# A scan ahead of routed experts: y products with two heads as moving columns, and routing steps spread over other pairs

## The chip, the cores and the metric

The kernel runs on one core of a Trainium2 chip. The metric is the device time in microseconds. A core has five engines with a queue each: TensorE (PE; its weight loads are listed as PEld), VectorE (DVE), ScalarE (ACT), GpSimd (POOL) and SyncE (SP), which here only issues DMAs. The trace gives for any stretch the clock that TensorE was granted, as a share of 2.4 GHz: 1.00 is 2.4 GHz, 0.50 is 1.2 GHz, and what lies between is a stretch that saw both.

## The reference, cut to what matters

```python
# part 1: a chunked state-space scan; x (4, 8, 768, 32), B and C (4, 8, 768, 16), a (4, 8, 768)
cum = np.cumsum(log(a) in the chunk, axis=-1)
M = (Cc @ Bc.T) * exp(cum_i - cum_j) * causal
y = M @ xc + (Cc @ state) * exp(cum)          # intra + inter
state = exp(sum) * state + sum_j Bc_j * exp(cum_last - cum_j) * xc_j
# part 2: tokens (3072, 256) = y of all heads side by side; 8 experts
expert_idx = token_ids * 2654435761 % 8
out[mask_e] = relu(x[mask_e] @ w1[e]) @ w2[e]  # w1 (8, 256, 1024), w2 (8, 1024, 256)
```

## The kernel before

**The scan.** Sequences are cut into units of T = 64 tokens. A pair k covers 256 tokens of one batch (four units, two chunks of 128); there are 12 pairs, three to each of four batches. In a prologue the decays are made (`fac`), B and C are multiplied by them (`rows_part`), transposed on PE (`turn_bc`) and brought back to SBUF (`evict_bc`, as `bts` for B and `ces` for C; `ces` has two copies, in each of which the other head of a pair of heads is zero). `back(k)` transposes B once more for the states, `dstates` makes the state's growth of each unit in PSUM, `states` adds it up on DVE (`z`) and writes the scaled state on POOL (`sps`). `gram(k)` makes the products of C and B in PSUM, and `masked(k)` copies their causal part into SBUF (`m_sb`, two copies on DVE).

**The y products.** `inter(k, swap)` (L561) multiplies `ces` by the state, `intra(k, t)` (L571) `m_sb` by x. Both take one head at a time: 32 moving columns a matmul, and each fp32 matmul runs as two passes, so that the trace shows twice as many. All of a pair's y lies in two PSUM banks (BY and BY + 1), from which `y_evict` (L578) copies it in one ACT instruction; `y_store` sends it to `y_tokens` in DRAM.

**Order in a pair.** The loop over k issues: loads of x, B and C; the store of pair k - 1; `turn_bc` and `evict_bc` of the next batch; `inter(k, 0)`, `dstates` and `states` of pair k + 1, `intra(k, 0)`, again `dstates` and `states`, `intra(k, 1)`; `rows_part` of a later batch on POOL; `inter(k, 1)`, `y_evict(k)`, `gram(k + 1)`, `piece(k)`, `back(k + 2)`, `masked(k + 1)`. Each engine runs its instructions in this order, which nothing rearranges.

**Routing.** `piece(k)` holds a step of the routing of tokens to experts: mask and count of tokens (`rt_mask`, `rt_count`, pair 0), ranks of experts and sizes (`rt_prefix`, pair 1; `rt_place`, `rt_rank`, pair 2), slots (`rt_slot_*`, pairs 3 and 4), then in quarters the one-hot table of lanes (`rt_lanes`, L390, 24 instructions on POOL), the one-hot table of slot tiles (`rt_tiles`, DVE) and their product on PE (`rt_table`, L404), and the list of token numbers (`to_index`). At the end of pair 9 POOL issues the indirect gathers of the five early token tiles (`gather`, L448), and PE turns three of them at the end of pair 10 and two at the end of pair 11 (`turn_x`, L456). The halves of w1 of the first experts are loaded by SP in pairs 8 to 10.

**The experts** follow (`up`, `down`, `sums_*`, `put`); the change does not touch them. `filler(n)` (L177) issues n bf16 products of zeros with 512 columns into an unused bank; `ident` is the identity for PE's transposes.

Of the kernel before, what the change touches and what calls it, by code (L numbers as in the profile page):

```python
# [25 lines left out]
def kernel(  # L26
# [148 lines left out]
    def filler(n):  # L175
        for _ in range(n):
            pe.matmul(out=ps[:, 3], lhsT=fill16[:, 0:P], rhs=fill16, start=True, stop=True)  # L177
# [19 lines left out]
    filler(3)  # L197
# [28 lines left out]
    def evict_bc(b, part, bank, eng):  # L226
        k = 0
        for i, r0, r1 in PARTS[part]:
            src = ps[:, bank, k * P:(k + r1 - r0) * P].rearrange("q (r p) -> q r p", p=P)
            k += r1 - r0  # L230
            if i == 0:
                o = bts[b].rearrange("q (p r) -> q r p", r=R)[:, r0:r1]
# [5 lines left out]
            for e in range(2):  # L238
                o = ces[b][:, e].rearrange("q (p r) -> q r p", r=R)[:, r0:r1]
                if eng[e] is act:  # L240
# [31 lines left out]
    def rt_ids():  # L272
# [4 lines left out]
        pe.transpose(out=ps[:, BQ, 0:NCH], in_=eid_r, identity=ident[0:NCH, 0:NCH])  # L277
        dve.tensor_copy(out=eid, in_=ps[:, BQ, 0:NCH])
# [31 lines left out]
    def rt_place(n, poh):  # L310
        pick = small("pick", [P, 3, E, E])
        for i in range(3):
            dve.tensor_tensor(out=pick[:, i], in0=poh, in1=ctab[:, i].unsqueeze(1).to_broadcast([P, E, E]), op=OP.mult)
        dve.tensor_reduce(out=sel, in_=pick, axis=AX.X, op=OP.add)
        who = small("who", [P, E, E])
        dve.tensor_tensor(out=who, in0=poh.rearrange("q e k -> q k e"), in1=iota_e.unsqueeze(1).to_broadcast([P, E, E]),
                          op=OP.mult)
        whof = small("whof", [P, E])
        dve.tensor_reduce(out=whof, in_=who, axis=AX.X, op=OP.add)
        dve.tensor_copy(out=place_i, in_=whof)  # L320
        half = sel[:, 0]
# [12 lines left out]
        dve.tensor_tensor(out=ovt, in0=tend, in1=ovt, op=OP.subtract)  # L334
        dve.tensor_scalar(out=ovt, in0=ovt, scalar1=float(P), scalar2=float(NSL), op0=OP.mult, op1=OP.add)
        dve.scalar_tensor_tensor(out=ovt, in0=half, scalar=-2.0, in1=ovt, op0=OP.mult, op1=OP.add)
        dve.tensor_tensor(out=ovt, in0=ovt, in1=sel[:, 1], op=OP.subtract)
        dve.tensor_tensor(out=ovt, in0=ovt, in1=sel[:, 2], op=OP.subtract)
# [42 lines left out]
    CG = 6  # L381

    def rt_lanes(eng, q):
        c = slice(q * CG, (q + 1) * CG)
        if eng is dve:
            dve.tensor_tensor(out=laneoh[:, c], in0=iota_n.unsqueeze(1).to_broadcast([P, CG, P]),
                              in1=lane[:, c].unsqueeze(2).to_broadcast([P, CG, P]), op=OP.is_equal)
            return
        for i in range(q * CG, (q + 1) * CG):
            eng.tensor_scalar(out=laneoh[:, i], in0=iota_n, scalar1=lane[:, i:i + 1], scalar2=None, op0=OP.is_equal)  # L390
# [214 lines left out]
    dstates(0, 1)  # L605
    masked(0)
    states(0, (1, 2, 3))
    back(1)

    state = {}  # L610

# [434 lines left out]
```

## Time and profile before

| | us |
|---|---|
| three runs: median (lowest to highest) | 316.12 (312.74 to 316.29) |
| the profiled execution, its own time | 310.52 |
| its span, first to last instruction | 308.8 |
| TensorE's mean granted clock over the span | 0.834 |
| PE busy, PEld busy | 262.1, 233.7 |
| DVE, ACT, POOL busy | 171.0, 85.7, 190.3 |

A busy PE is not a PE at its peak, since matmuls are pipelined and their ends are modelled; what a row of matmuls takes is read from the starts of its first and of what follows it. The share of busy time is a mean over a prologue, a scan and an expert part that have different limits. In the rows below a name with two arrows is output<-input, and what stands in square brackets is the idle time ahead of the instruction and who ended it.

### The profile page before, as it was taken

To read this page: it belongs to the slowest core of one execution; us is meant where nothing else is said; L and a number is where in the kernel's file an instruction comes from. 1 tells how busy PE (TensorE), PEld (TensorE's weight loads), DVE (VectorE), ACT (ScalarE), POOL (GpSimd) and SP (SyncE) were. 2 spreads that over 40 slices of the span, in tenths; PEclk is the share of its full clock that TensorE was granted. 3 is DMA by queue.
4 is the path that set the end of the run, shared out by engine and by line. 5 is a ranking of instruction groups with operands and counts; after the bars stand their busy time and mean duration, and the time that the engine had idled before them with its cause. 6 is when DMAs were issued, how large, how long until landed. Compare 5 with 4: busy or idle time off the path is not lost.

```text
span 308.8 us, 8166 instructions
## 1 busy us (share of the span) xinstructions
PE 262.1 (85%) x3373; PEld 233.7 (76%) x3374; DVE 171.0 (55%) x343; ACT 85.7 (28%) x183; POOL 190.3 (62%) x240
## 2 busy tenths in 40 slices
PE   8559968899899897888899899699699899999840
PEld 3338747787678686768889899699699898999730
DVE  6542673855343104796666647775763866656420
ACT  4412532234411246031112140141142240332100
POOL 3423366689927228989849739869359589272440
PEclk9755995559655569797999999799799999999985
DMA  8913474335544359350370551280170140410110
GB/s 185 219 23 70 89 157 102 58 75 101 114 112 126 106 139 363 111 187 3 88 269 20 175 167 34 46 312 18 20 269 20 65 142 17 152 38 17 51 41 14
DMA packets 55098, 33.30 MB, mean 108 GB/s; under 512 B 34906, under 2 KB 49394, under 8 KB 55060
## 3 DMA queue, kind: packets, MB, share of 16 engines
q1 hardware_dynamic: 52480, 26.22, 32.1%
q0 software_dynamic: 2400, 6.43, 6.2%
q8 instruction: 27, 0.44, 0.6%
q10 hardware_dynamic: 180, 0.12, 0.2%
q14 instruction: 11, 0.09, 0.1%
HBM read 26.47 MB, written 6.42 MB: 107 GB/s over the span
## 4 chain that ended last, share of the span: by engine, by line
PE 34%; DVE 9%; DMA 7%; POOL 2%; issue 1%; ACT 0%; POOLq 0%; DVEq 0%
PE ps L818 17%; PE ps L776 15%; DMA out_dram<-o_sb,idx_out 7%; DVE t L737 1%; DVE u L795 1%; DVE t L736 1%; PE ps L456 1%; PE ps L844 1%; DVE t L735 1%; DVE t L754 1%; DVE t L747 1%; DVE du L835 1%; DVE xT L836 1%; DVE t L738 1%; POOL s L727 1%
## 5 line engine op out<-in xcount | busy, mean ns | idle before, releaser
L853 POOL DMA_INDIRECT out_dram<-o_sb,idx_out x25 | 27.1, 1085 | 36.4 <-ACT o_sb L849 29.7
L448 POOL DMA_INDIRECT xg<-y_tokens,idx_in x25 | 27.2, 1086 | 30.7 <-PE ps L844 14.0
L510 POOL TENSOR_SCALAR sp<-z,g_sb 128x64 f32<-128x64 f32 x44 | 19.4, 453 | 36.8 <-DVE z L518 25.8
L776 PE MATMUL ps<-t,s 128*128 128x202 f32 (+7 forms) x192 | 38.5, 337 | 3.6 <-DVE t L736 2.3
L776 PEld LDWEIGHTS ps<-t,s 128*128 128x128 f32 x192 | 33.0, 195 | 5.0 <-DVE t L736 2.6
L818 PE MATMUL ps<-t,s 128*128 128x202 f32 (+7 forms) x192 | 34.9, 326 | 0.0
L818 PEld LDWEIGHTS ps<-t,s 128*128 128x128 f32 x192 | 31.3, 189 | 0.0
L571 PE MATMUL ps<-x_t,m 64*64 64x32 f32 x768 | 22.6, 269 | 4.5 <-DVE m L536 3.7
L776 PE MATMUL ps<-xT,w 128*128 128x202 f32 (+7 forms) x128 | 26.3, 343 | 0.0
L798 ACT ACTIVATE hx<-hx 128x404 f32<-128x404 f32 (+7 forms) x16 | 8.4, 525 | 62.2 <-DVE hx L797 62.2
L571 PEld LDWEIGHTS ps<-x_t,m 64*64 64x64 f32 x768 | 19.5, 190 | 8.0 <-DVE m L536 4.1
L561 PE MATMUL ps<-sp,ce 32*64 32x32 f32 x704 | 22.9, 266 | 1.1 <-issue 1.0
L561 PEld LDWEIGHTS ps<-sp,ce 32*64 32x64 f32 x704 | 19.5, 184 | 5.5 <-issue 4.0
L776 PEld LDWEIGHTS ps<-xT,w 128*128 128x128 f32 x128 | 23.0, 202 | 0.5 <-ACT p1e L783 0.5
L776 PE MATMUL ps<-t,w 128*128 128x202 f32 (+7 forms) x64 | 15.5, 368 | 9.0 <-DVE u L795 8.9
L518 DVE SCALAR_TENSOR_TENSOR z<-z,g_sb,ps 128x64 f32<-128x64 f32 x40 | 11.2, 279 | 20.4 <-PE ps L497 17.2
L776 PEld LDWEIGHTS ps<-t,w 128*128 128x128 f32 x64 | 11.4, 206 | 11.4 <-DVE u L795 11.4
L536 DVE COPY_PREDICATED m<-cmask,ps 128x512 f32<-128x512 int32 x24 | 16.0, 718 | 6.8 <-PE ps L528 6.8
L578 ACT ACTIVATE y_sb<-ps 128x512 f32<-128x512 f32 x12 | 7.2, 597 | 42.9 <-PE ps L561 42.9
L462 ACT ACTIVATE xT<-ps 128x256 f32<-128x256 f32 x25 | 9.4, 377 | 20.4 <-PE ps L456 20.4
L390 POOL TENSOR_SCALAR laneoh<-iota,lane 128x128 bf16<-128x128 f32 x24 | 14.2, 608 | 0.3 <-DVE stile L379 0.3
L776 PE MATMUL ps<-xT,s 128*128 128x202 f32 (+7 forms) x64 | 14.4, 355 | 0.0
(181 smaller groups left out, 553.4 us busy)
## 6 DMA issues: line engine op xcount, KB each, us to landing
w<-in_moe_w_dram SPq DMA_DIRECT2D x16, 512.0 KB, 4.8
w<-in_moe_w_dram SPq DMA_DIRECT2D x8, 1024.0 KB, 5.6
x_t<-in_x_dram SPq DMA_DIRECT2D x24, 128.0 KB, 3.3
y_tokens<-y_sb SPq DMA_DIRECT2D x24, 128.0 KB, 2.4
bc<-in_B_dram SPq DMA_DIRECT2D x4, 384.0 KB, 4.1
bc<-in_C_dram SPq DMA_DIRECT2D x4, 384.0 KB, 4.3
xg<-y_tokens,idx_in POOLq DMA_INDIRECT x25, 4.6
out_dram<-o_sb,idx_out POOLq DMA_INDIRECT x25, 2.5
```

What stands on the lines that cost most here:

```text
L390: eng.tensor_scalar(out=laneoh[:, i], in0=iota_n, scalar1=lane[:, i:i + 1], scalar2=None, op0=OP.is_equal)
L448: pool_e.indirect_dma_start(out=xg[k], out_offset=None, in_=y_dram[0:n, :], in_offset=bass.IndirectOffsetOnAxis(ap=idx_in[:, k:k + 1], axi ...
L462: act.activation(o, i, AF.Copy)
L510: pool_e.tensor_scalar(out=sps[k][:, n], in0=zs["z"], scalar1=g_sb[:, un - 1:un], scalar2=None, op0=OP.mult)
L518: dve.scalar_tensor_tensor(out=z, in0=zs["z"], scalar=g_sb[:, un - 1:un], in1=d, op0=OP.mult, op1=OP.add)
L536: dve.copy_predicated(out=m[:, t], mask=mk, data=ps[:, 0:G, t * P:(t + 1) * P])
L561: pe.matmul(out=o, lhsT=ces[b][r, e, c:c + T], rhs=sps[k][r, n, e * D:(e + 1) * D], start=first, stop=False, skip_group_check=True)
L571: pe.matmul(out=o, lhsT=m_sb[k % 2][u * T:(u + 1) * T, t, h // 2, e * T:(e + 1) * T], rhs=xs[2 * k + t][u * T:(u + 1) * T, h], start=first ...
L776: pe.matmul(out=ps[:, bank, i * n:(i + 1) * n], lhsT=lhs[:, (q0 + i) * P:(q0 + i + 1) * P], rhs=rhs, start=(first and i == 0), stop=True, ...
L798: act.activation(hq(2), hq(2), AF.Relu)
L818: pe.matmul(out=ps[:, bank, 0:n], lhsT=lhs(q), rhs=rhs(q), start=(first and q == 0), stop=True, skip_group_check=True)
L853: st = pool_e.indirect_dma_start(out=out[:], out_offset=bass.IndirectOffsetOnAxis(ap=idx, axis=0), in_=o_sb, in_offset=None, bounds_check= ...
```

## The change

**y products.** `inter` takes `sps[k][r, n]` whole and `intra` x of both heads of a pair: 64 moving columns. Half of the columns of each product are not used. The y of a pair now fills both banks, and `y_evict` picks the used columns in two ACT instructions, one for each bank.

**Prologue.** Fifteen more fillers in all stand among the prologue's products, besides the two that are added behind the decays' sums (3 become 5). The token ids are made on DVE before the rows products, `rt_turn` turns them later, all four rows products of batch 0 stand on DVE, the evictions are dealt out anew, and `gram(0)` comes before `dstates(0, 0)`. `rt_mask` and `rt_count` move into the prologue. The eviction of `bts` writes its output in order and reads PSUM with a stride.

**Routing.** The steps stand in other pairs: `rt_prefix` 0, `rt_place` 1, `rt_over` and `rt_past` 2, `rt_rank` and the register load 3, `rt_slot_a` to `c` 4, `rt_slot_d` 5, `rt_tiles` and the first lanes 6, further lanes 7 to 9, tables 7, 8, 9 and 9, the index list 9. The picks of `rt_place`, all of `rt_past` and `rt_slot_c` and half of the tile table move from DVE to POOL; the lanes move from POOL to DVE, in four instructions of 768 elements. The early gathers are issued at the end of pair 10, and the five turns stand together at the end of pair 11.

```diff
-    filler(3)
+    filler(5)
...
-                o = bts[b].rearrange("q (p r) -> q r p", r=R)[:, r0:r1]
+                o = bts[b].rearrange("q (p r) -> q p r", r=R)[:, :, r0:r1]
+                src = src.rearrange("q r p -> q p r")
...
-            dve.tensor_tensor(out=pick[:, i], in0=poh, ...)
+            pool_e.tensor_tensor(out=pick[:, i], in0=poh, ...)
...
-        o = ps[hh * T:(hh + 1) * T, BY + u, t * P + h4 * D:t * P + (h4 + w) * D]
+        o = ps[hh * T:(hh + 1) * T, BY + u, (t * 4 + h4) * 2 * D:(t * 4 + h4 + 1) * 2 * D]
...
-                    pe.matmul(out=o, lhsT=ces[b][r, e, c:c + T], rhs=sps[k][r, n, e * D:(e + 1) * D],
+                    pe.matmul(out=o, lhsT=ces[b][r, e, c:c + T], rhs=sps[k][r, n],
...
-                                  rhs=xs[2 * k + t][u * T:(u + 1) * T, h], start=first, stop=True, skip_group_check=True)
+                                  rhs=xs[2 * k + t][u * T:(u + 1) * T, h - e:h - e + 2], start=first, stop=True, skip_group_check=True)
...
-        act.activation(ysb[k].rearrange("q t u s -> q u t s"),
-                       ps[:, BY:BY + 2, 0:2 * P].rearrange("q u (t s) -> q u t s", t=2), AF.Copy)
+        o = ysb[k].rearrange("q t u (g e d) -> q u t g e d", g=2, e=2)
+        for u in range(2):
+            i = ps[:, BY + u].rearrange("q (t g w) -> q t g w", t=2, g=2)
+            i = i[:, :, :, 0:4 * D].rearrange("q t g (e d) -> q t g e d", e=4)[:, :, :, 0:4:3]
+            act.activation(o[:, u], i, AF.Copy)
...
+    eid_r = rt_ids()
     rows_part(dve, 0, 0, 0, 4)
-    rows_part(pool_e, 0, 1, 0, 2)
     rows_part(dve, 0, 0, 4, 6)
-    rows_part(pool_e, 0, 1, 2, 6)
+    rows_part(dve, 0, 1, 0, 2)
+    rows_part(dve, 0, 1, 2, 6)
     turn_bc(0, 0, BT)
-    evict_bc(0, 0, BT, (act, act))
-    rt_ids()
+    filler(2)
+    evict_bc(0, 0, BT, (act, act, act))
     turn_bc(0, 1, BY)
-    evict_bc(0, 1, BY, (act, dve))
+    filler(1)
+    evict_bc(0, 1, BY, (act, dve, dve))
+    turn_bc(0, 2, BY + 1)
+    evict_bc(0, 2, BY + 1, (act, act, dve))
+    rt_turn(eid_r, BT)
+    filler(3)
     back(0)
-    turn_bc(0, 2, BY + 1)
-    evict_bc(0, 2, BY + 1, (act, dve))
     rows_part(pool_e, 1, 0, 0, 4)
     decays_of_units()
+    filler(3)
+    gram(0)
+    rt_mask()
     dstates(0, 0)
+    filler(2, BY + 1)
     states(0, (0,))
-    gram(0)
     dstates(0, 1)
     masked(0)
     states(0, (1, 2, 3))
+    rt_count(BT)
+    filler(4, BY + 1)
     back(1)
...
-        if k == 9:
+        if k == 10:
             for q in EK:
                 gather(q, early=True)
-        if k >= 10:
-            for q in EK[(k - 10) * 3:(k - 9) * 3]:
+        if k == 11:
+            for q in EK:
                 turn_x(q)
```

DVE in the prologue, from the rows products to the causal copies of pair 0 (`eid` are the token ids, `rg` the sums for the units' decays, `m` the masked products). Before:

```order
L208 TENSOR_TENSOR rows_257<-bc,fac 128x512
L208 TENSOR_TENSOR rows_257<-bc,fac 128x256
L274 TENSOR_SCALAR eid_i<-tok 24x128
L276 CAST eid_r<-eid_i 24x128
L278 COPY eid<-ps 128x24
L243 TENSOR_SCALAR ce<-ps,par 128x2x128
L243 TENSOR_SCALAR ce<-ps,par 128x4x128
L471 TENSOR_TENSOR rg<-bg,cm 128x48
L472 TENSOR_TENSOR rg<-bg,cum 128x48
L516 COPY z<-ps 128x64
L536 COPY_PREDICATED m_117<-cmask,ps 128x512 x2
```

and of the change:

```order
L275 TENSOR_SCALAR eid_i<-tok 24x128
L277 CAST eid_r<-eid_i 24x128
L208 TENSOR_TENSOR rows_264<-bc,fac 128x512
L208 TENSOR_TENSOR rows_264<-bc,fac 128x256
L208 TENSOR_TENSOR rows_267<-bc,fac 128x256
L208 TENSOR_TENSOR rows_267<-bc,fac 128x512
L244 TENSOR_SCALAR ce<-ps,par 128x2x128 x2
L244 TENSOR_SCALAR ce<-ps,par 128x4x128
L282 COPY eid<-ps 128x24
L478 TENSOR_TENSOR rg<-bg,cm 128x48
L479 TENSOR_TENSOR rg<-bg,cum 128x48
L285 TENSOR_TENSOR mask_233<-eid,iota_142 128x192
```

The ids stand ahead of the rows products, two rows products come over from POOL, and the id transpose's copy stands behind the evictions.

POOL from pair 5 to pair 8 (`sp` are the scaled states, `rows` the decayed B and C of a later batch, `laneoh` the lanes). Before:

```order
L510 TENSOR_SCALAR sp<-z,g_sb 128x64 x3
L208 TENSOR_TENSOR rows_1163<-bc,fac 128x512
L390 TENSOR_SCALAR laneoh<-iota_146,lane 128x128 x6
L510 TENSOR_SCALAR sp<-z,g_sb 128x64 x4
L208 TENSOR_TENSOR rows_1163<-bc,fac 128x256
L208 TENSOR_TENSOR rows_1308<-bc,fac 128x256
```

and of the change, from pair 4 on:

```order
L363 TENSOR_TENSOR g_237<-g_237,sel 128x192
L365 TENSOR_SCALAR half_1066<-sel 128x8
L371 TENSOR_TENSOR g_1068<-g_1068,ovt 128x192
L372 TENSOR_TENSOR val<-val,sel 128x192
L373 TENSOR_TENSOR g_237<-g_237,g_1068 128x192
L376 TENSOR_TENSOR val<-val,g_237 128x192
L377 TENSOR_TENSOR val<-val,mask_233 128x192
L517 TENSOR_SCALAR sp<-z,g_sb 128x64 x3
L208 TENSOR_TENSOR rows_1169<-bc,fac 128x512
L517 TENSOR_SCALAR sp<-z,g_sb 128x64 x4
```

The lanes are gone from POOL, and the last slot steps, two of them from DVE, now stand between the states and the rows product that the transposes of pair 6 wait for.

DVE from pair 1 to pair 3, before:

```order
L313 TENSOR_TENSOR pick<-poh,ctab 128x64 x3
L314 TENSOR_REDUCE sel<-pick 128x24
L316 TENSOR_TENSOR who<-poh,iota_142 128x64
L319 TENSOR_REDUCE whof<-who 128x8
L320 CAST place_i<-whof 128x8
L323 TENSOR_TENSOR shift<-sel,pin 128x8
L324 TENSOR_SCALAR shift<-shift 128x8
```

and of the change:

```order
L318 TENSOR_REDUCE sel<-pick 128x24
L323 TENSOR_REDUCE whof<-who 128x8
L324 CAST place_i<-whof 128x8
L543 COPY_PREDICATED m_117<-cmask,ps 128x512 x2
L523 COPY z<-ps 128x64
L525 SCALAR_TENSOR_TENSOR z<-z,g_sb,ps 128x64 x3
L329 TENSOR_TENSOR shift<-sel,pin 128x8
L330 TENSOR_SCALAR shift<-shift 128x8
```

The picks have left DVE, and the masked copies and states of a pair stand between the placing and the sizes, where before all of it ran ahead of the masked copies of pair 3.

## Rows read from the trace of the kernel before

**Rows 1.** Stretches from pair to pair: length, busy time (instructions) by engine, PEclk, DMA.

```profile
core 0: us, PE busy (x) PEld busy (x) DVE busy (x) ACT busy (x) POOL busy (x), PEclk, DMA share, GB/s
...
24.09:32.27 8.18, 7.93 (x185) 6.44 (x184) 2.72 (x7) 2.53 (x4) 2.87 (x6) 0.51 0.37 87
32.27:37.30 5.03, 4.69 (x191) 3.70 (x190) 3.04 (x9) 2.56 (x5) 2.46 (x4) 1.00 0.43 76
37.30:42.96 5.66, 4.81 (x200) 3.81 (x199) 4.29 (x12) 3.08 (x4) 2.88 (x6) 1.00 0.73 159
42.96:53.17 10.21, 7.27 (x184) 5.99 (x183) 5.95 (x25) 2.07 (x3) 5.77 (x13) 0.64 0.48 104
...
69.41:74.94 5.53, 4.81 (x189) 3.96 (x188) 3.42 (x11) 2.07 (x3) 4.90 (x10) 0.98 0.44 81
...
95.93:104.75 8.82, 7.87 (x191) 5.88 (x190) 3.10 (x7) 1.75 (x4) 5.69 (x8) 0.50 0.70 197
...
110.70:121.32 10.62, 10.53 (x51) 9.72 (x50) 2.58 (x4) 6.21 (x13) 6.07 (x6) 0.84 0.95 291
```

**Rows 2.** Instructions in order of time, PE, ahead of both rises of the clock.

```profile
30.30 0.37 PE L286 MATMUL ps<-mask,upto 128*128 128x192 bf16 x1
...
67.50 0.43 PE L404 MATMUL ps<-tab,laneoh 128*128 128x50 bf16 x6
```

**Rows 3.** Instructions in order of time, all engines, in the prologue.

```profile
7.97 1.46 DVE L208 TENSOR_TENSOR rows<-bc,fac 128x512 f32<-128x512 f32 x2 [1.41 <-ACT fac L200]
...
9.35 1.07 DVE L274 TENSOR_SCALAR eid_i<-tok 24x128 int32<-24x128 int32 x1
...
11.58 0.22 PE L277 MATMUL ps<-ident,eid_r 24*128 24x24 f32 x1 [2.20 <-DVE eid_r L276]
...
15.13 1.15 ACT L241 ACTIVATE ce<-ps,par 128x512 f32<-128x512 f32 x1 [0.47 <-PE ps L223]
16.32 1.11 DVE L243 TENSOR_SCALAR ce<-ps,par 128x512 f32<-128x512 f32 x1 [1.63 <-ACT ce L241]
...
20.20 0.65 PE L497 MATMUL ps<-x_t,bn 64*32 64x64 f32 x16
```

**Rows 4.** Instructions in order of time, PE, behind two waits.

```profile
47.20 1.08 PE L571 MATMUL ps<-x_t,m 64*64 64x32 f32 x32 [2.94 <-DVE m L536]
...
78.72 0.47 PE L561 MATMUL ps<-sp,ce 32*64 32x32 f32 x18 [1.02 <-issue]
```

**Rows 5.** One stretch of ten microseconds, columns as in the first group.

```profile
90.00:100.00 10.00, 10.00 (x286) 8.27 (x286) 4.33 (x11) 0.98 (x2) 5.63 (x8) 0.50 0.53 137
```

**Rows 6.** Costliest groups: busy, mean ns of one, then idle before and its releaser.

```profile
L578 ACT ACTIVATE y_sb<-ps 128x512 f32<-128x512 f32 x12 | 7.2, 597 | 42.9 <-PE ps L561 42.9
...
L390 POOL TENSOR_SCALAR laneoh<-iota,lane 128x128 bf16<-128x128 f32 x24 | 14.2, 608 | 0.3 <-DVE stile L379 0.3
```

**Rows 7.** PE in order of time, passes at the low and at the high clock.

```profile
25.67 1.08 PE L571 MATMUL ps<-x_t,m 64*64 64x32 f32 x32
...
39.51 0.43 PE L497 MATMUL ps<-x_t,bn 64*32 64x64 f32 x16
39.86 0.67 PE L571 MATMUL ps<-x_t,m 64*64 64x32 f32 x32
40.46 0.60 PE L561 MATMUL ps<-sp,ce 32*64 32x32 f32 x27
...
41.53 0.44 PE L486 MATMUL ps<-ident,bt 128*128 128x128 f32 x2
```

**Rows 8.** DVE in order of time, a sum of 512 elements.

```profile
116.94 0.69 DVE L718 TENSOR_TENSOR s<-s,w 128x512 f32<-128x512 f32 x1
```

**Rows 9.** Groups of instructions by form, 24 to 110 us, POOL.

```profile
L208 POOL TENSOR_TENSOR rows<-bc,fac 128x512 f32<-128x512 f32 x5 | 5.3, 1055 | 0.0
...
L361 POOL TENSOR_TENSOR g<-g,ovt 128x192 f32<-128x192 f32 x1 | 0.5, 508 | 0.5 <-DVE g L360 0.5
```

**Rows 10.** Early gathers: POOL in order of time; DMA issues with us to landing.

```profile
98.60 0.99 POOL L448 DMA_INDIRECT xg<-y_tokens,idx_in  x1 [0.30 <-issue]
...
xg<-y_tokens,idx_in POOLq DMA_INDIRECT x25, 4.6
```

## What the change should do to the time

> **What bounds the kernel now.** I read the table of stretches first, cut at the first inter product of each pair. The scan's pairs 0 to 9 take 71.84 us (24.09 to 95.93), ahead of them lies a prologue to 24.09, behind them two pairs with the turning of the early tiles (95.93 to 110.70), then the expert part. The reader is to see that equal pairs do not take equal time: with a granted clock of 0.98 to 1.00 (2.4 GHz) they take 5.03, 5.66 and 5.53 us, pair 0 at 0.51 (nearly all of it at 1.2 GHz) 8.18, and pair 3 10.21 at 0.64 [rows 1]. PE is the engine that waits least, so the clock is what a pair costs. It is high from about 32 to 46 and from about 69.6 to 80 us, 24 us of the scan's 87.
>
> Second, what PE did before the clock changed. It rose at about 32 and at about 69.6 us, in both places behind count or table products with 128x128 weights [rows 2] and the transposes of 128x128 that follow them. It fell after idle stretches: the wait for the token ids in the prologue [rows 3], the wait for DVE's routing in pair 3 (2.94 us, PE idle from 44.3 to 47.2) and the 1.02 us wait in pair 7 [rows 4]. But from 90 to 100 us PE is busy 10.00 of 10.00 us and the clock stays at 0.50 [rows 5].
>
> **A, prologue.** Before, DVE makes the token ids between its second rows product and its evictions (from 9.35, two instructions of about 1 us), PE's in-order queue stands behind the id transpose until 11.58, and the last eviction ends at 17.43, since DVE's half waits for ACT's [rows 3]. After, DVE makes the ids in the 1.4 us that it is idle before the rows; if the ids come late, the rows wait, which I price at 0 to 1 us. DVE then makes all four rows products: twice 1.46 us from 7.97, so to 10.9; four transposes at the high clock take 0.7: 11.6; ACT's eviction 1.15: 12.8; DVE's 1.11: 13.9. That is 3.5 us earlier. From there to the gram's end before took 2.8 us at the low clock; at the high one, with three fillers of 512 columns, I take 1.9. Masks, states and the transposes to pair 0 took 3.9; 0.4 less for back and turn at the high clock, but dstates now stand between gram and masks (0.4): 3.9. The four fillers behind the count lie beside the masks. Pair 0 starts at about 19.8 instead of 24.09: **4.3**. If the clock is low anyway, the three fillers before the gram cost 1.3 and 4.3 becomes 2.2; if the bt eviction, now written in order, takes 0.60 as ACT's 128x512 copy of y does [rows 6], half a microsecond more is won: 4.8.
>
> **B, the y products.** No matmul is added; 64 columns move instead of 32. 32 intra passes are busy for 1.08 us at the low clock and 0.67 at the high one, where their starts span 0.60, 18.8 ns each. The nearest rows at the high clock: dstates moves 64 columns in 0.35 us for 16 passes, 22 ns; and 64 passes, half inter with 32 columns and half gram with 128, span 1.07 us, 17 ns each [rows 7]. So a wider pass costs between 0 and 4 ns more, on the 123 passes of a pair (768 and 704 in 12): 0 to 0.5 us. I take 0.24, the upper price for intra alone, since inter has the gram's shape of weights (32x64); at the low clock 0.3. [...]
>
> What the wider products are worth is the clock. No row shows it, so I bound it: nothing, or the high clock in all pairs. I take the high end, since the stalls before which it fell are reduced (C), the prologue is filled up, and with the clock once high, pairs 1, 2 and 6 stayed high even with 32 columns. At the high clock the three pairs average 5.41, of which the mask wait of pair 2 and the table wait of pair 6 are about 0.3 together per pair; 5.1 + 0.24 = 5.35. Pairs 8 and 9 lack the transposes of 128x128 (0.6): 4.7. So 8 x 5.35 + 2 x 4.7 = 52.2.
>
> **C, routing and lanes.** The 14.2 us of slot lanes (24 of 608 ns) leave POOL [rows 6]. DVE gets four of 768 elements instead; by its 128x512 sum of 0.69 [rows 8] each is 1.0, the 600-element table 0.8. DVE is free in a high pair from about 3.1 us after its start (states done) to 5.3, when masks must begin or the next intra waits: 2.2 us. Lanes (1.0 and up to 0.8 more) fit. What does not: in pair 1 the picks move to POOL behind its 1.06 us rows product [rows 9]; DVE waits there with the masks behind it, and PE's intra behind them: 0.9. In pair 4 a similar wait of DVE: 0.2. In pair 5 the last slot steps (now five on POOL, 0.51 each and 2.6 in all [rows 9]) push the states and the rows product back, and PE's transposes wait for rows: 1.1. Pair 9 has two tables, two additions and the indices: 0.2. Table products, 0.2 each: 0.8. Sum 3.2, so the ten pairs take 55.4 and **16.4** are gained. Pair 3's 2.94 us wait is in this, as rt_place and rt_over are now in two pairs and rt_past is on POOL. The y eviction, 0.60 in one part, comes in two; it lies beside gram and transposes, and uncovered would cost at most another 0.60 a pair.
>
> **D, the end of the scan.** The gathers move from pair 9 to pair 10, and the five turns all to the end. POOL issues one per 1.29 us, and each lands 4.6 us after its issue [rows 10]; from 2.6 us into pair 10, when POOL has pair 11's states, the fifth is issued at 7.8, lands at 12.4, and its transposes end at 12.9. The products of the two pairs, about 3.9 and 3.0, end at 6.9, so PE waits 6 us for gathers. Before, 14.77: **1.9** gained. The expert part follows as it is: its up products started at the low clock before (0.84 in that stretch [rows 1]), and after this wait they will again. 0, at best 2.
>
> **Sum.** 4.3 + 16.4 + 1.9 = 22.6 off the profiled execution's 310.5: 287.9. The three runs' median, 316.12, lies 1.8% above that execution; scaled by it, 293. I name 290, 0.9% up and between them, and give the rivals' times with the same 0.9%, against a before of 313.
>
> **Rivals.** (1) The clock goes as before: the columns change nothing and it is high in four of ten pairs. For it: 90 to 100 us, all busy, all low [rows 5]. Then the prologue gives 3, pair 3's stall 3, pairs 6, 7 and 4 some 2.5 (lanes, DVE's waits), and the wide columns cost 0.24 to 0.3 in 12 pairs, 3.3: 5 gained: 308. [...]
>
> (2) The other side: the clock falls in the prologue and never rises in the scan. Place: any gap before pair 0, and then nothing like the count product and transposes in a row, since the count has moved out of pair 0. Pairs 0 to 7 then cost 8.3 each, 8 and 9 7.3: 81 against 71.84, 9.2 lost; the prologue still gains 2.2 and the end nothing: 320. It decides from about seven low pairs on. Against it: the transposes and tables still come in every batch, and the fillers.
>
> (3) Wide columns are paid in full: 123 passes x 18.8 ns more in 12 pairs, 28 us instead of 2.9: 316. Against it: the gram and dstates passes [rows 7].
>
> (4) Waits across DVE and POOL are longer than in C, each dropping the clock: three or four pairs low at 2.7 each (8.18 against 5.41): 300.
>
> **Chances.** Forecast 0.64, (4) 0.14, (1) 0.12, (2) 0.06, (3) 0.04. The forecast's own range is 281 to 297: 4 us from the base, 6 from pairs 0.5 us shorter or longer. With (4) and the lower part of (1), 281 to 305. Two per cent (6.3 us) is about what a measurement here can tell. Faster: forecast, (4), half of (1): 0.84. Same: the rest of (1) and (3): 0.10. Slower: 0.06.
>
> **What would show it.** A: the first inter products at 19 to 21 us, no idle PE from 9.4 to 11.6. B: granted clock near 1.00 in pairs 0 to 9 with starts of y passes 19 to 23 ns apart; clocks of 0.50 in stretches with a busy PE make it wrong, pass starts of 35 ns at the high clock rival (3). C: POOL without lanes, PE waiting for masks in pair 2 (after the picks) and for rows at pair 6, none over 1.5 us; a wait of 3 us there is rival (4). D: PE idle between turns, paced at 1.3 us. If the clock is high and the time still over 300, the loss is in D or in the expert part, which I took as unmoved.

## The result, and the profile after

The changed kernel takes **297.74 us** (median of 4 runs, 296.58 to 298.93) against 314.43 for the kernel before on the same chip: a ratio of **0.957, with a 95% interval of 0.945 to 0.969**. On a second chip the unaltered changed kernel stood at 0.955 (0.950 to 0.961). The forecast was 290 with a range of 281 to 305: the sign and the range hold. But 297.74 lies just above the 281 to 297 that the prediction gave to the forecast alone; the room up to 305 was there for rival 4 and part of rival 1. By the medians 16.7 us are gained where the forecast had 23 (313 to 290); by the two profiled executions, 310.52 before and 298.93 after, it is half: 11.6 us, where the sum had 22.6.

The stretches come first, cut as in [rows 1] at the first inter product of each pair (with the columns explained there); the last four rows are the two last pairs, the five turns, and the expert part.

```profile
0.00:20.61 20.61, 17.14 (x176) 8.55 (x176) 12.73 (x35) 7.46 (x14) 6.00 (x44) 1.00 0.93 160
20.61:25.93 5.32, 4.83 (x183) 3.86 (x182) 3.13 (x10) 1.60 (x5) 3.00 (x6) 1.00 0.42 92
25.93:31.26 5.33, 4.82 (x191) 3.64 (x191) 2.13 (x6) 2.63 (x7) 2.98 (x7) 1.00 0.61 116
31.26:38.43 7.17, 5.03 (x200) 3.93 (x199) 5.85 (x20) 3.08 (x5) 3.50 (x10) 1.00 0.79 159
...
43.32:51.13 7.81, 6.25 (x192) 4.69 (x191) 2.70 (x9) 2.53 (x7) 5.62 (x13) 0.79 0.50 91
...
68.59:76.83 8.24, 5.20 (x201) 3.92 (x200) 2.58 (x8) 2.77 (x4) 2.30 (x4) 0.90 0.69 158
76.83:84.89 8.06, 7.76 (x192) 6.22 (x191) 3.68 (x10) 1.04 (x3) 2.30 (x4) 0.50 0.18 49
84.89:91.32 6.43, 6.43 (x189) 5.39 (x191) 2.52 (x9) 1.04 (x3) 2.55 (x4) 0.50 0.46 116
91.32:95.44 4.12, 3.10 (x137) 2.69 (x128) 1.37 (x3) 0.00 (x0) 3.00 (x3) 0.88 0.61 163
95.44:99.75 4.31, 2.23 (x16) 1.28 (x11) 0.00 (x0) 2.08 (x6) 1.00 (x1) 0.92 0.65 151
99.75:297.20 197.45, 167.46 (x987) 159.95 (x986) 117.35 (x191) 50.16 (x124) 132.64 (x105) 0.94 0.33 107
```

Pair 0 starts at 20.61 (24.09 before). Pairs 0 to 9 take 64.28 us (71.84 before). Nine of the ten run mostly or wholly at the high clock, and pair 0, which took 8.18 at 0.51, takes 5.32 at 1.00. But pairs 2, 4 and 8 take 7.2 to 8.2 us although PE is busy for only 5.0 to 6.3 of them, and from 75 us on the clock is low again: pairs 9 and 10 are busy almost without a gap at 0.50. What stands in pairs 2, 4 and 8 is a kind of wait of which the kernel before had two in its scan, 0.45 and 1.02 us long. These are PE's waits by what ended them, from 20 to 95 us:

```profile
PE ps L535 <- issue: 5.1, 3, 3.0
PE ps L578 <- issue: 2.1, 3, 1.5
PE ps L223 <- POOL rows L208: 1.7, 4, 0.9
PE ps L578 <- DVE seen L688: 0.7, 1, 0.7
PE ps L578 <- DVE m L543: 0.6, 1, 0.6
```

"Issue" means that nothing which the profile shows ended the wait. Eight of these waits lie in the scan, in the middle of runs of like passes; five of them in order of time (L535 is the gram, L578 the intra products, L568 the inter products):

```profile
28.82 0.21 PE L578 MATMUL ps<-x_t,m 64*64 64x64 f32 x1 [0.34 <-issue]
...
37.24 0.45 PE L535 MATMUL ps<-ce,bt 32*64 32x128 f32 x8 [1.52 <-issue]
...
46.27 0.57 PE L578 MATMUL ps<-x_t,m 64*64 64x64 f32 x22 [1.53 <-issue]
...
65.98 0.52 PE L568 MATMUL ps<-sp,ce 32*64 32x64 f32 x20 [0.36 <-issue]
...
75.34 0.70 PE L535 MATMUL ps<-ce,bt 32*64 32x128 f32 x8 [3.04 <-issue]
```

Up to pair 9 they cost 7.5 us (0.49, 0.34, 1.52, 1.53, 0.24, 0.36, 3.04). Set against the 8.9 us that pairs 0 to 9 lack (64.28 instead of 55.4) that is the larger part, and most of the experiments are about them.

### The profile page after: what moved, and what is told of

Its sections match the earlier page's. It is cut to its first block, busy times and chain, and to the rows that moved or that the text cites. A ratio compares the mean times of both kernels' runs of the same rounds, so it can differ in the third digit from the quotient of the medians.

```text
span 297.2 us, 8179 instructions
## 1 busy us (share of the span) xinstructions
PE 250.3 (84%) x3391; PEld 219.9 (74%) x3391; DVE 169.1 (57%) x329; ACT 83.5 (28%) x194; POOL 181.9 (61%) x227
## 4 chain that ended last, share of the span: by engine, by line
PE 43%; DVE 11%; DMA 7%; POOL 2%; ACT 1%; issue 1%; POOLq 0%; DVEq 0%
PE ps L795 21%; PE ps L837 17%; DMA out_dram<-o_sb,idx_out 7%; PE ps L463 2%; DVE t L755 2%; DVE u L814 2%; DVE t L756 1%; DVE t L754 1%; PE ps L863 1%; DVE t L773 1%; DVE t L757 1%; DVE du L854 1%; DVE xT L855 1%; ACT xT L469 1%; POOL s L746 1%
## 5 line engine op out<-in xcount | busy, mean ns | idle before, releaser
L517 POOL TENSOR_SCALAR sp<-z,g_sb 128x64 f32<-128x64 f32 x44 | 21.0, 487 | 36.0 <-DVE z L525 25.2
L795 PEld LDWEIGHTS ps<-t,s 128*128 128x128 f32 x192 | 34.1, 201 | 5.4 <-DVE t L755 3.2
L837 PEld LDWEIGHTS ps<-t,s 128*128 128x128 f32 x192 | 31.3, 189 | 0.0
L578 PE MATMUL ps<-x_t,m 64*64 64x64 f32 x768 | 19.9, 241 | 3.6 <-issue 2.1
L795 PE MATMUL ps<-t,w 128*128 128x202 f32 (+7 forms) x64 | 14.2, 344 | 9.3 <-DVE u L814 9.2
L568 PE MATMUL ps<-sp,ce 32*64 32x64 f32 x704 | 19.9, 246 | 0.7 <-issue 0.7
L578 PEld LDWEIGHTS ps<-x_t,m 64*64 64x64 f32 x768 | 15.7, 148 | 6.4 <-issue 3.1
L568 PEld LDWEIGHTS ps<-sp,ce 32*64 32x64 f32 x704 | 16.1, 152 | 4.7 <-issue 3.6
L590 ACT ACTIVATE y_sb<-ps 128x256 f32<-128x256 f32 x24 | 7.9, 381 | 36.3 <-PE ps L568 36.3
L535 PE MATMUL ps<-ce,bt 32*64 32x128 f32 x384 | 12.7, 319 | 5.1 <-issue 5.1
L837 PE MATMUL ps<-hx,s 128*128 128x202 f32 (+7 forms) x64 | 12.0, 329 | 2.8 <-DVE xT L855 2.8
```

The source lines that it names most:

```text
L517: pool_e.tensor_scalar(out=sps[k][:, n], in0=zs["z"], scalar1=g_sb[:, un - 1:un], scalar2=None, op0=OP.mult)
L535: pe.matmul(out=ps[u * T:(u + 1) * T, g, t * P:(t + 1) * P].rearrange("q (e i) -> q e i", e=2), lhsT=bts[b][r, c:c + T], rhs=ces[b][r, :, ...
L568: pe.matmul(out=o, lhsT=ces[b][r, e, c:c + T], rhs=sps[k][r, n], start=first, stop=False, skip_group_check=True)
L578: pe.matmul(out=o, lhsT=m_sb[k % 2][u * T:(u + 1) * T, t, h // 2, e * T:(e + 1) * T], rhs=xs[2 * k + t][u * T:(u + 1) * T, h - e:h - e + 2 ...
L795: pe.matmul(out=ps[:, bank, i * n:(i + 1) * n], lhsT=lhs[:, (q0 + i) * P:(q0 + i + 1) * P], rhs=rhs, start=(first and i == 0), stop=True, ...
L837: pe.matmul(out=ps[:, bank, 0:n], lhsT=lhs(q), rhs=rhs(q), start=(first and q == 0), stop=True, skip_group_check=True)
```

## The experiments

Eleven altered kernels, and the change itself once more, ran on three chips; each ratio is against the kernel before on the same chip.

**1. The wide columns, alone and taken away.** Two kernels: the change with products of 32 columns again, and the kernel before with nothing but the wide ones.

```diff
 # change with narrow products: intra, inter and the eviction as before
-rhs=xs[2 * k + t][u * T:(u + 1) * T, h - e:h - e + 2]
+rhs=xs[2 * k + t][u * T:(u + 1) * T, h]
-rhs=sps[k][r, n]
+rhs=sps[k][r, n, e * D:(e + 1) * D]
 # before with wide products: the same lines the other way round
```

> The changed kernel with one thing undone: the y products move 32 columns again (y layout and eviction as before); prologue, fillers and routing stay changed. Theory 1, that the wider products hold and bring back the clock: it falls to 0.50 at the first longer wait of the scan and stays there for most of it, as in the kernel before; the scan from pair 0 to pair 10, 64.3 us in the changed kernel, takes 72 to 76, and the time is 304 to 310. Theory 2, that fillers and shorter waits do it and the columns are idle work: granted clock as in the changed kernel, the time 295 to 299, rather lower for the passes saved.

> The kernel before with one part of the change alone: y products with 64 columns, the y layout and the eviction in two parts; prologue and routing as before. Theory 1: the prologue ends low as before, but the dense products then raise the clock within a pair or two, and it comes back within a pair after each wait (pair 3's 3 us, pair 7's); pairs 4, 5, 8 and 9 at 1.00 in place of 0.50, 300 to 305 us. Theory 2: clock as before, 0.50 from 46 to 69 and from 80 us on, and 3 us more for the wider passes: 314 to 318.

Narrow: 303.07 us, 0.970 (0.962 to 0.979), just under the range of its theory 1; its scan from pair 0 to pair 10 takes 67.3 us, not 72 to 76. Wide alone: 306.95 us, 0.981 (0.974 to 0.988), between the ranges of its two theories. The layout and the eviction of y go with the columns in both. The five rows are the same stretch, 20 to 100 us, of the kernel before, the change with narrow products, the kernel before with wide ones, the change without its added fillers (experiment 2), and the change.

```profile
20.00:100.00 80.00, 71.16 (x2072) 57.33 (x2060) 42.53 (x123) 24.99 (x40) 48.66 (x89) 0.65 0.44 95
```

```profile
20.00:100.00 80.00, 73.88 (x2225) 60.56 (x2224) 38.90 (x103) 24.16 (x42) 43.24 (x78) 0.66 0.50 106
```

```profile
20.00:100.00 80.00, 65.49 (x2108) 52.32 (x2100) 42.73 (x123) 25.65 (x50) 49.70 (x91) 0.78 0.45 101
```

```profile
20.00:100.00 80.00, 64.05 (x2233) 50.78 (x2232) 39.02 (x103) 25.80 (x56) 43.20 (x78) 0.86 0.53 114
```

```profile
20.00:100.00 80.00, 66.57 (x2237) 52.05 (x2236) 39.00 (x103) 26.18 (x58) 43.69 (x80) 0.87 0.54 113
```

The third number from the end is the granted clock, of one execution each. Without the wide columns it is that of the kernel before, 0.66 against 0.65, however well the rest is ordered; with them alone it is 0.78; with both 0.87. So the clock comes with the wide columns, as the prediction's B says, and the other parts bring 9 us without it (312.08 to 303.07 on this chip). In time the columns are worth 5 us alone (312.08 to 306.95) and about 4 us within the change: 303.07 against the 299.24 of experiment 2 on the same chip, whose kernel also lacks the fillers. The two intervals overlap a little (0.962 to 0.979 and 0.952 to 0.964); the times themselves do not (301.41 to 305.46 and 298.01 to 300.19).

What the columns cost can be read in pair 8 of the change, at the high clock:

```profile
69.58 0.70 PE L578 MATMUL ps<-x_t,m 64*64 64x64 f32 x32
70.21 0.43 PE L504 MATMUL ps<-x_t,bn 64*32 64x64 f32 x16
```

The next passes start 0.63 us after the 32 intra passes did, 19.7 ns a pass against 18.8 with 32 columns [rows 7]. Rival 3, by which they would be paid in full, is out.

**2. The fillers.** The 17 fillers that the change adds in the prologue are left out.

```diff
-    filler(5)
+    filler(3)
 ...
-    filler(4, BY + 1)      # and the five other calls between the rows and pair 0
```

> The changed kernel without its 17 added fillers, everything else changed. Fillers are needed to start the scan high: the clock falls in the prologue's gaps and pair 0 starts at 22 to 23 us instead of 20.6, the wide products raise the clock in pair 0 or 1: 300 to 302 us. Fillers are idle work: pair 0 starts at 20.6 or earlier and the time is 296 to 298.

299.24 us, 0.958 (0.952 to 0.964): between the two ranges that were expected, and no difference from the change that can be measured. Its clock is low from 16.6 to 26.8 us, so pair 0 takes 7.2 us instead of 5.3, and then high for 51 us; what was lost at the start came back by pair 3, which starts at 38.53 against 38.43: it has no issue wait between pair 0 and 42.1 us, where the change has three (0.49, 0.34 and 1.52).

**3. Are they instruction blocks?** One row suggests what the waits without a releaser are. The page lists a DMA queue that moves instructions:

```profile
q8 instruction: 27, 0.44, 0.6%
```

27 packets with 0.44 MB are 16 KB each, and PE's 3,391 matmuls and 3,391 weight loads over 27 packets are 125.6 pairs in each. The waits fit that size. These rows count PE's matmuls from the start of the span into five of its waits (the number behind PE's busy time):

```profile
0.00:24.50 24.50, 20.86 (x349) 11.64 (x350) 14.57 (x41) 8.68 (x17) 7.88 (x48) 1.00 0.83 141
0.00:28.60 28.60, 24.52 (x476) 14.51 (x477) 17.71 (x49) 10.64 (x21) 9.67 (x52) 1.00 0.81 144
0.00:36.50 36.50, 30.64 (x731) 19.13 (x731) 22.25 (x63) 14.48 (x28) 14.79 (x62) 1.00 0.79 142
0.00:45.50 45.50, 38.06 (x985) 25.02 (x986) 27.27 (x77) 17.98 (x36) 21.23 (x79) 1.00 0.78 144
...
0.00:74.00 74.00, 61.84 (x1877) 43.49 (x1877) 43.84 (x116) 29.14 (x58) 40.38 (x110) 0.98 0.68 126
```

349, 476, 731, 985, (1240, 1622) and 1877 differ by multiples of 127.3. If that is so, 64 pairs more ahead of the scan must move each wait 64 pairs back in the program.

```diff
-    filler(16)
+    for _ in range(80):
+        pe.matmul(out=ps[:, 3, 0:102], lhsT=fill16[:, 0:P], rhs=fill16[:, 0:102], ...)
```

> The first 16 fillers of the prologue, of 512 columns each, are replaced by 80 of 102 columns: as many columns, but 64 more pairs of a weight load and a matmul ahead of the scan. Theory (PE waits at the edge of a block of about 127 such pairs, until the queue named instruction has brought the next): the waits without a releaser stay at PE's running counts (about 731, 986, 1622 and 1877 pairs, plus or minus 3, or others that differ from these by multiples of 127), so that in the program they come 64 pairs earlier: the wait ahead of the last eight gram passes of pair 9 is gone, and where there is one it stands among the y products or state passes of pair 8. Rival (they belong to a place in the program, a buffer or a semaphore that the profile does not show): the same eight gram passes of pair 9 and the same 22 y products of pair 4 wait again, at counts of about 1941 and 1050.

These are counts into waits of that kernel, and its wait in pair 8:

```profile
0.00:25.90 25.90, 21.99 (x476) 16.38 (x477) 16.64 (x48) 10.65 (x21) 8.94 (x51) 1.00 0.82 154
...
0.00:34.20 34.20, 28.20 (x731) 21.18 (x731) 19.94 (x59) 13.82 (x26) 13.13 (x60) 1.00 0.76 141
...
0.00:73.40 73.40, 60.31 (x1877) 46.76 (x1877) 42.12 (x116) 28.46 (x56) 39.14 (x109) 0.95 0.66 127
```

```profile
73.87 0.49 PE L579 MATMUL ps<-x_t,m 64*64 64x64 f32 x8 [0.94 <-issue]
```

Eleven waits fall on counts 476, 604, 731, 858, 986, 1113, 1368, 1495, 1750, 1877 and 2132: the old counts and others of the same grid, in other places of the program. (Two more, of 0.2 us, lie off it, at 2355 and 2360, during the gathers; the last section has more of that kind.) The gram of pair 9 does not wait any more; the eight last intra passes of the second half of pair 8 do, as expected. This kernel ran once, in 303.92 us, so its time says nothing. The kernel before fits the grid to within three counts: its 0.45 and 1.02 us waits stand at 601 and 1620. The grid's 127.3 pairs lie near the 125.6 to a 16 KB packet. So these waits stand at the edges of instruction blocks, and the 1.02 us wait was never the slot lanes'.

**4. What makes a block late.** At the longest wait, from 72.30 to 75.34 us, the instruction packet comes late. The first view is the DMA of 69.2 to 72.9 us, the second that of 73.0 to 73.2:

```profile
q1 hardware_dynamic: 617, 0.68, 73.1%
q14 instruction: 1, 0.01, 0.5%
issues: line engine op xcount, KB each, median us to landing
w<-in_moe_w_dram SPq DMA_DIRECT2D x1, 512.0 KB
```

```profile
q8 instruction: 1, 0.02, 29.3%
```

In the first no packet of q8 starts, and the engines are 73% taken by the data queue, mostly the first early half of w1. The packet starts 0.7 us into the wait, at 73.02, when the load has just ended, and takes 0.94 us (29.3% of 16 engines' 0.2 us); PE goes on 1.4 us after its end. At all eight waits of the scan PE goes on 1.3 to 1.7 us after the end of a q8 packet. Four kernels move that load (the fourth is in experiment 6). In the first, the three early halves of w1 come after the last store of y:

```diff
-        if 8 <= k < 11:
-            load_w1(k - 8, 0)
     y_store(NP - 1)
+    for p in range(3):
+        load_w1(p, 0)
```

> The changed kernel with the three early halves of w1 (512 KB each, issued in pairs 8 to 10) issued behind the last store of y instead. Theory A, that PE's 3.0 us wait in the middle of the gram products of pair 8 (72.3 to 75.3 us, no releaser) is its next block of instructions coming late behind the first of these loads: the wait is under 0.5 us, the clock stays at 1.00 through pairs 9 and 10, and the scan ends some 8 us earlier; up to 4 of them go back because the up products wait for w1 at the start of the expert part: 291 to 294 us. Rival: the wait has nothing to do with the loads: it stays at 3 us at the same place, and the late loads cost 2 to 5 us: 300 to 303.

295.57 us (293.82 to 300.22), 0.944 (0.938 to 0.950). The wait in the same place, by the profiled execution, which at 300.22 is the longest of the six:

```profile
73.61 0.45 PE L535 MATMUL ps<-ce,bt 32*64 32x128 f32 x8 [0.71 <-issue]
...
97.48 3.73 PE L795 MATMUL ps<-xT,w 128*128 128x202 f32 x10 [2.13 <-DMA w<-in_moe_w_dram]
```

0.71 instead of 3.04, though not under the 0.5 that theory A had, and a new wait of 2.13 at the start of the expert part, which had its first half of w1 ready before. The q8 packet for this edge now starts 4.1 us after the one before it, and not 5.9 as in the change. The second and third kernel spread the loads instead:

```diff
-        if 8 <= k < 11:
-            load_w1(k - 8, 0)
+        if 5 <= k < 11:                       # four pieces of 128 KB for each half
+            load_w1_part((k - 5) // 2, (k - 5) % 2, 0)
+            load_w1_part((k - 5) // 2, (k - 5) % 2, 1)
 # third kernel, also:
-            load_bc(b + 2, j)                 # 384 KB
+            load_bc_part(b + 2, j, 0)         # 192 KB here, 192 KB at the end of the pair
```

> The three early halves of w1, 512 KB each and issued in pairs 8, 9 and 10 before, are issued in twelve pieces of 128 KB, two in each of pairs 5 to 10; nothing else. Theory (a block of PE's instructions stands in line behind a long transfer): the 3.04 us wait in pair 8 falls under 1.5, the scan ends 1.5 to 3 us earlier, and the expert part starts without the 2.13 us wait that the late issue had: 0.940 to 0.950 of before, 2 to 4 us below the unaltered changed kernel. Rival (the size does not matter, only that bytes move in pairs 8 to 10): the waits of pairs 8 to 10 keep their sum of about 3 us, and the time stays within 1 us of the unaltered one.

> As the run before, and each load of B or C for the batch after the next (384 KB) in two halves by heads, the second at the end of the pair. Theory: the two waits of 1.5 us in pairs 2 and 4 fall to under 1 us each, 1 to 2 us less than with the w1 pieces alone, and the low clock after them goes or shortens. Rival: the bytes in flight around the block's edge stay as many, the waits keep 1.2 us or more and the time is the same within 1 us.

> The changed kernel unaltered, as the measure for the two spread versions that run beside it on the same chip: 0.957 of the kernel before, with PE's waits that no releaser ends in the middle of runs of like matmuls (0.3 to 3.0 us each, the longest with eight gram passes of pair 9 still to come).

Spread: 299.79 us, 0.951 (0.948 to 0.954), against 302.29, 0.955 (0.950 to 0.961), for the unaltered change on that chip; with B and C in halves too 300.66, 0.957 (0.953 to 0.960). The wait of pair 8 was 1.94 and 1.40 us against 2.20, so the first of the two missed the 1.5 that was expected, and it was followed by others of 1.06, 0.46 and 1.79 us at the next edges. In the waits the rival had it, since the bytes move in these pairs in any case, and their sum of 5.3 us is even above its 3. In time 2.5 us by the medians speak for the theory, but the intervals overlap. In the third kernel the waits of pairs 2 and 4 are 1.12 and 0.50 us (0.69 and 1.32 in the unaltered change on that chip): no gain in the first, some in the second, none in the time.

Without the load a wait is left. In the kernel with late halves, whose DMA engines are 30% taken by stores of y in the four microseconds before, the edges of pairs 8 to 10 still wait 0.71, 0.78, 0.19 and 0.79 us. A block does not last long at the high clock: between the change's waits at 28.82 and 37.24 two of them ran in 8.42 us, 1.52 of which were the wait, 3.45 us each. At the low clock the same edges are mostly free: in the change, pairs 9 and 10 pass three of them (2004, 2131 and 2258; 5.62 us from the first to the second, 80.91 to 86.53) without a listed wait, and the two waits of the kernel before came at 1.00. With a load in front they are not. At a clock of 0.50 the kernel of experiment 2 waited 1.78 us at its edge 2003, that of experiment 3 0.94, and that of experiment 6 with the turns alone 1.09, each time behind a packet that started as the load of an early half of w1 ended. In the first that is at 79.94 us:

```profile
82.30 0.58 PE L568 MATMUL ps<-sp,ce 32*64 32x64 f32 x10 [1.78 <-issue]
```

```profile
78.00:79.00 1.00, 1.00 (x40) 0.72 (x35) 0.08 (x2) 0.00 (x0) 0.44 (x1) 0.52 0.86 221
...
80.00:83.00 3.00, 1.22 (x38) 1.03 (x43) 0.88 (x2) 0.00 (x0) 1.19 (x2) 0.50 0.00 0
```

The DMA engines, 0.86 busy before (the last number but one), are idle in the wait. So part of the wait in pair 8, the 0.71 us that are left without the load, goes with the higher clock, and a load adds up to 2.6 us to it (3.30 less 0.71); how early before its edge a packet has to start stays open.

**What the clock does behind that wait.** The same gram of pair 9 waits in eight profiled executions. Where it waited 2.20 us (the unaltered change, second time), 3.04 (the change; the turns of experiment 6) or 3.30 (the gathers of experiment 5), the clock fell behind it and was 0.50 from 79 to 87 us; where it waited 0.71, 1.12, 1.40 or 1.94, it was 0.99 to 1.00 in that stretch. The change itself, and the one with spread w1:

```profile
79.00:87.00 8.00, 7.70 (x206) 6.16 (x202) 4.18 (x13) 1.04 (x3) 2.30 (x4) 0.50 0.29 64
```

```profile
79.00:87.00 8.00, 5.55 (x245) 4.28 (x244) 3.00 (x11) 1.70 (x5) 2.86 (x5) 1.00 0.32 72
```

206 matmuls against 245 in the same 8 us. In these executions the late block goes with two costs, the wait and the clock behind it. (It is not so everywhere: waits of 0.7 to 1.8 us in pair 2 were followed by no fall in any of them, and the change's wait of 1.53 us in pair 4 was, from 47.9 to 51.3 us. The length of the wait alone does not decide it.)

**5. Lanes and gathers put back.** Two kernels: the slot lanes on GpSimd again, and the gathers at the end of pair 9 with three turns in pair 10 and two in pair 11.

```diff
 # lanes
-        dve.tensor_tensor(out=laneoh[:, c], ...)
+        for i in range(q * CG, (q + 1) * CG):
+            pool_e.tensor_scalar(out=laneoh[:, i], ...)
 # gathers
-        if k == 10:
+        if k == 9:
             for q in EK:
                 gather(q, early=True)
```

> The changed kernel with the slot lanes back on GpSimd, six instructions of 608 ns for each quarter (as in before) instead of one of 0.94 us on VectorE, at the same places in pairs 6 to 9. Theory (the 1.02 us wait that before had among its wide passes came from the edge of an instruction block and not from the lanes, and 3.65 us of GpSimd lie beside a pair of 5 us or more): within 1 us of the unaltered changed kernel, 0.953 to 0.960 of before. Rival (the lanes hold up the rows or the states on GpSimd, as the prediction had it): waits of 0.9 us or more for the states' or the table's operands in pairs 6 to 9, 2 to 4 us slower.

> The changed kernel with the five gathers issued at the end of pair 9, three of their turns in pair 10 and two in pair 11, as before the change. Theory of the prediction (GpSimd, busy with gathers for 6.5 us, hands over the states of pair 11 late): 1 to 2 us slower than the changed kernel, with a wait of PE's wide passes of pair 11 for GpSimd. Rival (the place of the gathers makes no difference, since at the low clock of pairs 10 and 11 PE takes as long as GpSimd): within 0.7 us.

Lanes: 302.58 us, 0.961 (0.949 to 0.974). In PE's waits from 60 to 85 us stands what the rival named, and not my theory that the lanes would not matter:

```profile
PE ps L223 <- POOL rows L208: 2.5, 2, 2.2
PE ps L411 <- POOL laneoh L397: 1.5, 4, 0.4
```

4.0 us of waiting for GpSimd, where the change has about 1.5 in these pairs. In time the difference to the change (0.955 and 0.957) lies within the intervals. Moving the lanes did take waits away, though not the one that I had put down to them.

Gathers: 299.92 us, 0.942 (0.928 to 0.956). Not slower than the change, so the 1 to 2 us that were expected of the prediction's D are not there; whether the old place is the better one the intervals leave open.

**6. The turns, and everything together.** In the change each turn at the end but the first waits for the eviction of the one before (0.66, 0.47, 0.47 and 0.47 us). One kernel alternates two banks and two engines; another does that, loads the first half of w1 in pair 6, and the two others after the last store.

```diff
-            for q in EK:
-                turn_x(q)
+            for i, q in enumerate(EK):
+                turn_x(q, (BT, BQ)[i % 2], (act, dve)[i % 2])
 # together, also:
-        if 8 <= k < 11:
-            load_w1(k - 8, 0)
+        if k == 6:
+            load_w1(0, 0)
     y_store(NP - 1)
+    load_w1(1, 0)
+    load_w1(2, 0)
```

> The changed kernel with its five turns of gathered rows at the end of the scan put alternately into two banks of the accumulator, and evicted alternately by ScalarE and VectorE; nothing else. Theory (at the end of the scan each turn waits only for the eviction of the one before, 0.47 us at either clock, four times): the turns take 2 to 2.5 us instead of 4.3 and the kernel gains 1.5 to 2.3 us. Rival (the landing of the gathers, 1.3 us apart, is what the turns would meet next): the turns wait for gathers and gain under 0.5 us.

> Two edits together: the turns as in the run before, and of the three early halves of w1 the first issued in pair 6 and the two others after the last store of y. Theory: the long wait of pair 8 falls to under 1 us as when all three were late, a wait of 1.5 to 3 us may come up at the next block edge after the load in pair 6, and the expert part finds its first half of w1 (no wait of 2.13 us): 0.935 to 0.945 of before, 3 to 5 us below the changed kernel. Rival (the expert part's two other halves, now late, stop it): a wait of 2 us or more for w1 within the first 10 us of the expert part, and no gain over the all-late version.

Turns: 301.36 us, 0.947 (0.933 to 0.961). They go from 4.31 us to 2.31:

```profile
102.36 0.76 PE L463 MATMUL ps<-ident,xg 128*128 128x128 f32 x4
103.48 0.66 PE L463 MATMUL ps<-ident,xg 128*128 128x128 f32 x4 [0.36 <-ACT xT L469]
104.39 0.44 PE L463 MATMUL ps<-ident,xg 128*128 128x128 f32 x2 [0.26 <-ACT xT L469]
104.67 1.53 PE L795 MATMUL ps<-xT,w 128*128 128x202 f32 x8
```

The step is right and 2 us long; the time shows it only within its interval, since this execution lost 3.1 us in pair 11 to another wait (below). Together: 298.79 us, 0.943 (0.932 to 0.954). The load in pair 6 made no wait at all, the gram of pair 9 waited 1.12 (under 1 was expected), and the expert part waited 2.55 us for a later half of w1, 5.8 us after its start: half the theory, half the rival, and no better than the all-late version at 0.944.

So three versions stand at 0.942 to 0.944, below the change's 0.955 and 0.957; only for the all-late one does the interval (0.9378 to 0.9495) lie just below that of the change measured again (0.9500 to 0.9607), and that on another chip; it overlaps the first one (0.945 to 0.969).

## Why the prediction was right, and where its sizes were off

| part | forecast gain | measured, profiled executions |
|---|---|---|
| A, prologue | 4.3 (pair 0 at 19.8) | 3.5 (24.09 to 20.61) |
| B and C, pairs 0 to 9 | 16.4 (to 55.4) | 7.6 (71.84 to 64.28) |
| D, end of the scan | 1.9 (to 12.9) | -0.1 (14.77 to 14.86) |
| expert part | 0 | 0.6 (198.1 to 197.45) |
| sum | 22.6 | 11.6 |

The sign and the named range hold, and for the range that is partly luck: the sum is twice what the profiled executions show, 297.74 lies outside the 281 to 297 of the forecast alone, and what opened the range that far was rival 4, which had the waits at other engines.

**A** held. Pair 0 starts at 20.61 in this execution, 18.8 to 20.7 in the eleven others that have the changed prologue (one of them without its fillers). The fillers, which the prediction counted as part of the clock's cover, are worth nothing that can be measured (experiment 2).

**B** was right in its mechanism and in its price: 19.7 ns a pass, 0.9 more and within the 0 to 4 ns bounds, and the clock comes with them (experiment 1). It was wrong in taking the high clock for all pairs. The mark that I set myself, a clock of 0.50 with a busy PE, is there from 76.8 to 91.3 us: PE is busy 14.2 of 14.5 us with wide columns and the clock does not come back. With the wide columns the high level was there more of the time, 0.87 against 0.66, and not all of it.

**C** is the step that was mis-sized. Its own waits came out about as forecast: 0.59 for the masks behind the picks (0.9 forecast), 0.26, 0.85 and 0.39 for rows (1.1), 0.30 for tables. The sum had no term for PE's instruction blocks, 7.5 us in pairs 0 to 9, nor for the low clock that followed the longest of them: pair 9 took 8.06 instead of 4.7, 3.4 more. 7.5 and 3.4 are more than the 8.9 us that are missing; the rest of the pairs was 2.0 better than forecast. The sign of this term stood in the rows that I read: the 1.02 us wait of pair 7 [rows 4] had "issue" behind it, in the middle of a run of like passes, and I counted it among the stalls that the change would reduce, pair 7's share in rival 1 as one of "lanes, DVE's waits". The change has more of such waits, not fewer: eight against two. That fits blocks that the high clock uses up sooner (3.45 us each, against 5.62 at 0.50). Rival 4 had the shape of this outcome, 300 us by three or four waits that each drop the clock, and the wrong engines: most of the waiting was not for VectorE or GpSimd.

**D** failed twice. In this execution PE never waited for gathers (in that of experiment 2 it did twice, 1.18 and 0.90 us), since pairs 10 and 11 took 10.55 us at a mostly low clock instead of 6.9; and the turns, which were to be paced by the landings, were paced by ScalarE, 0.47 to 0.66 us of waiting for each eviction. Putting the gathers back cost nothing that could be measured (experiment 5).

**The rivals.** The clock as before (308) and the clock low all scan (320) are out by the 0.87, columns in full (316) by the 19.7 ns.

## What to carry to other kernels

A wait in the middle of a run of like instructions, with no releaser, is worth counting: if the instruction counts at such waits differ by multiples of one number, suspect that the engine's own program arrives late, and test it by moving the counts by a known number of instructions, as in experiment 3. Price a large transfer also by the stretch of short instructions that it falls into (127 pairs of weight load and matmul ran in 3.45 us there), and not only by when its data are needed: here moving one took the longest wait from 3.04 to 0.71 us. Widening the moving columns cost 0.9 ns a pass here, and what it brought came through the clock, so it must be judged together with the waits behind which the clock fell again.

## What the runs showed of the hardware

The page of the change lists 27 packets with 0.44 MB, 16 KB each, on the queue that it calls instruction, and the eight waits without a releaser in its scan stand multiples of 127.3 pairs of weight load and matmul apart. At all eight PE goes on 1.3 to 1.7 us after the end of such a packet. An edge of this grid cost nothing at some places (2004, 2131 and 2258) and, over all runs, 0.2 to 3.3 us of waiting at others, mostly at a granted clock of 1.00. The change's longest, 3.04 us, stood behind a 512 KB load: its packet started at 73.02, when that had just ended, and with the load behind the last store the wait was 0.71.

What the shares of the clock are worth can be read in the change too. At 1.00 two fillers of 512 columns took 0.43 us, from the start of the first (10.25) to that of the product behind them (10.68): 2.4 columns a nanosecond. 32 intra passes took 0.63 us at 1.00 (69.58 to 70.21) and 1.06 at 0.50 (78.46 to 79.52).

One thing stays open. In seven of the eleven profiled executions of kernels that gather in pair 10, PE's first intra product of pair 11 waited 2.9 to 4.6 us; in the four others 0.7 to 1.0. In the kernel with spread w1, VectorE's read of one column in each of the two accumulator banks ahead of it (`seen`) was held up for 3.83 us by what the profile calls remote, although the inter passes that it waits for are recorded as ended by 88.7:

```profile
87.50 1.17 PE L575 MATMUL ps<-sp,ce 32*64 32x64 f32 x29
```

```profile
93.03 0.16 DVE L695 COPY seen<-ps 128x2 f32<-128x2 f32 x1 [3.83 <-remote]
```

It falls into the time in which GpSimd issues the five gathers, the count is not at a block's edge, and with the gathers in pair 9 it did not occur. There PE's intra passes of pair 10 paused five times instead, off the grid of block edges (0.25 to 0.96 us, from 88 to 92.7 us, while the gathers were issued or right behind them); short pauses off the grid, 0.2 to 1.1 us, stand at the gathers in five other executions too. In the profiled execution of the unaltered change on the second chip, 302.68 us against 298.93 on the first, the long wait is 3.74 us and not 0.68. What holds PE there was not tried.
